# Two visits per group at fixed FFN steps, stores on SP's queue, and a last group in halves, in a fused linear-attention and FFN kernel

## The chip, the cores and the metric

The kernel runs on one core of a Trainium2 chip. The metric is the device time of one execution, in microseconds (us). TensorE is called PE here, VectorE DVE, ScalarE ACT, GpSimd POOL and SyncE SP. PEld is the stream of weight loads of PE.

## The reference

Per batch and head a gated linear attention keeps a 48x48 state that decays by `alpha` and takes in one outer product per token. Its output, 3072 tokens by 384 features, goes through a two-layer feed-forward network (FFN) with an exact GELU.

```
state = zeros((B, H, D, D))                      # B 4, H 8, S 768, D 48
for t in range(S):
    state = alpha[:, :, t, :, None] * state + einsum('bhd,bhe->bhde', k[:, :, t], v[:, :, t])
    y[:, :, t] = einsum('bhd,bhde->bhe', q[:, :, t], state)
x = y.transpose(0, 2, 1, 3).reshape(3072, 384)
h = x @ w_in                                     # 384 x 2048
g = 0.5 * h * (1 + erf(h / sqrt(2)))
return g @ w_out                                 # 2048 x 384
```

## The kernel before

The tokens form 12 groups of 256, three to a batch, and each group has two units (u = 0 and 1), each with half of the heads, so there are 24 units. All arithmetic is float32; every factor of a large matmul is split in a high and a low part, so a product takes three matmuls.

**The attention of a unit.** DVE scans the decays forward (`pp`, line 283) and backward (`rp`, 304) and scales the keys (`akq`, 309). POOL scales the queries (`qk`, 299). PE then makes the scores (`scores`, 325). DVE masks them (`ss`, 340) and ACT copies their other part (`kn`, 334). PE writes the product inside chunks (`inside`, 399), the state sums (`sums`, 426) and the part outside chunks (`outside_part`, 487) into one PSUM tile, `ybank`. DVE adds the sums up to states (`chain`, 452 and 454). ACT casts the finished `ybank` to the high half of the FFN's input (`x_high`, 541) and DVE makes the low half (`x_low`, 545). After the last chunk of a batch no state is needed, so `chain` has three adds in the last group of a batch and four (the first may be a copy) elsewhere.

**A visit.** From unit 6 on, PE does its attention work in bundles: the visit of unit n holds `inside` of n, `sums` of n+1, `scores` of n+2 and `outside_part` of n, in this order. `inside` and `outside_part` write to one bank from different row tiles. For that reason a POOL memset of one column (`done`, 834), called the fence, waits for the sums and `outside_part` waits for the fence.

**The FFN.** A group takes 8 steps f = 0 to 7. Step f is `gemm1` (18 matmuls into `hp`, 572), two GELUs on ACT (`ghi`, 593, and in place on `hp`, 594), their difference on DVE (`glo`, 599), and `gemm2` (12 matmuls into two accumulators `acc` of 128 tokens, 620; the first 8 need only `ghi`, the last 4 need `glo`). The two `hp` buffers let the next `gemm1` run while ACT and DVE work. There is one pair of accumulators, so step 0 of a group waits in `gemm2` until DVE has copied the pair of the group before to `part` (639). A store then carries `part` to the output (645), on POOL's queue; for the last group on SP's and ACT's queues (641).

**The order.** A planner at build time plays all engines through with a table of costs (`COST`) and writes out the order of PE, DVE, ACT and SP; POOL's order follows the program. On PE an operation marked `late` (the visits) is taken when what it waits for has been done for at least `MARGIN`; otherwise FFN steps run. At run time each engine works through its list in this fixed order and waits on semaphores.

A last check (`total`, 1088) reads whether all decays are in the range that the fast path allows.

Of the kernel before, what the change touches and what calls it, by code (L numbers as in the profile page):

```python
# [30 lines left out]
LANES = 8  # L31
RATE, ALONE, LATENCY, SMALL, BEGIN = 350e3, 290e3, 2.1, 50e3, 2.2
MARGIN = 1.5
HOME = {0: 0, 1: 1, 2: 2, 4: 1, 5: 0, 6: 2, 8: 1, 9: 0, 10: 2, "s": 1}
X_GAP, Z_GAP, HI_GAP, LO_GAP, LATE_GAP = (128, 0, 192), 0, (64, 0), (0, 64), 0
COST = dict(
    scan=0.65, back=0.72, keys=0.65, q=1.35, qv=0.62, scores=1.0, kn=0.5, mask=0.62, inside=1.05, chain=1.15, outer=0.85, carry=0.26, last=0.34, last_p=0.15, sums=0.55, scaled=0.45,
    xh=0.6, xl=0.65, spread=0.62, check=0.95, load=0.46, fetch=0.46, u=0.92, c0=0.56, c1=0.9, c2=0.45, c3=0.95, c4=0.92,
    hi=0.84, lo=0.9, gemm1=2.12, gelu=0.58, minus=0.35, low=0.63, gemm2=2.1, part=1.1,
)  # L40
ORDER = "0 1 2 3 a b c d 4 e 5 f g 6 h 7 i j k l 8 m n o p"

# [2 lines left out]
def gla_then_gelu_ffn(ctx: ExitStack, tc: tile.TileContext, q, k, v, alpha, akq, w_in, w_out, out):  # L45
    nc = tc.nc
    B, H, D, S = q.shape
    NF, P, NK, _ = w_in.shape
    DM, DFF = NK * P, NF * P
    NT = B * S  # L50
    C = 128
    G = 2 * C
# [8 lines left out]
    NG = B * GPB  # L61
    NSB = GPB
# [34 lines left out]
    minus = const.tile([P, P], F32R, name="minus")  # L97
# [29 lines left out]
    done = const.tile([P, 64], F32, name="done")[:, :1]  # L127
# [13 lines left out]
    for half in range(2):  # L141
        r = slice(half * CS, (half + 1) * CS)
        nc.gpsimd.affine_select(
            out=mask[r],
# [10 lines left out]
    wi_hi, wi_lo, wo_hi, wo_lo = (  # L155
        [const.tile([P, 2, DM], F32R, name=f"{n}{f2}") for f2 in range(NF2)] for n in ("wih", "wil", "woh", "wol")
    )
# [189 lines left out]
    def turned_over(g, b):  # L347
        return g >= NSB and b == 1
# [125 lines left out]
    def outside_part(g, u):  # L474
        d = cur[g, u]
        for c in range(NCH // 2):
            for i in range(2):
                for bb, h in ((0, 0), (0, 1), (1, 0), (1, 1)):
                    b = bb if g >= NSB else bb ^ h
                    j = 2 * c + b  # L480
                    if g % GPB == 0 and j == 0:
                        continue
                    r = slice(h * DP, h * DP + D)
                    o0 = (h ^ turned_over(g, b)) * DP
                    o = slice(o0, o0 + D)
                    t = (2 * i + c) * CS
                    ins = nc.tensor.matmul(  # L487
                        ybank[o, b, t : t + CS],
                        lhsT=states[u][j][r, i],
                        rhs=d["qs"][r, i, j, :CS],  # L490
                        start=False,
                        stop=True,
                        skip_group_check=True,
                    )
                    tc.add_manual_dep(
                        ins.ins,
                        (d["chain"] if g < NSB else d["fence"]).ins.name,
                        mybir.DependencyInfo(mybir.DependencyClass.Sync, mybir.DependencyReason.DATA),
                        reason="row tiles of one bank",
                    )  # L500
# [3 lines left out]
    def x_tiles(g):  # L504
# [4 lines left out]
        else:  # L509
            if g in range(XB):  # L510
                gap(ffn, X_GAP[HOME[g]], f"gap_x{g}")
            x = ffn.tile([P, NK, 2, G], F32R, tag=f"x{HOME[g]}", bufs=1, name=f"x{g}")
        xt[g] = x[:, :, 0], x[:, :, 1]
# [99 lines left out]
    started = set()  # L613

    def gemm2(g, f, ghi, glo, acc, first, last, done, n0=None):
        for k in range(2):
            for t in range(2):
                for j in range(2):
                    for a, w in (((ghi, wo_hi[f]), (ghi, wo_lo[f])), ((glo, wo_hi[f]),))[k]:
                        nc.tensor.matmul(  # L620
                            acc[t],
                            lhsT=a[:, j, t * C : (t + 1) * C],
                            rhs=w[:, j, :],
                            start=(first and j == 0 and k == 0 and w is wo_hi[f]),
                            stop=(last and j == 1 and k == 1),
                        )
        EARLY = tuple(range(NSB))
        if not last:
            return

        def evacuate():
            o = parts[0 if g == "s" else g % NSB]
            for t in range(2):
                if g in started:
                    nc.vector.tensor_tensor(out=o[:, t], in0=o[:, t], in1=acc[t], op=ALU.add)
                elif g in EARLY or t == 1 and g == NG - 1:
                    nc.scalar.copy(o[:, t], acc[t])
                else:
                    nc.vector.tensor_copy(o[:, t], acc[t])  # L639
                if g == NG - 1:  # L640
                    (nc.scalar if t else nc.sync).dma_start(out[g * G + t * C : g * G + (t + 1) * C, :], o[:, t])
            started.add(g)
            if done and g != NG - 1:
                rows = out[g * G : (g + 1) * G, :] if n0 is None else out[bass.ds(n0, G), :]
                nc.gpsimd.dma_start(rows.rearrange("(t p) e -> p t e", p=C), o)  # L645

        return evacuate

# [84 lines left out]
    n_units = NG * NU  # L733

    class Op:
        made = 0

        def __init__(self, eng, cost, fn, deps=(), rank=0.0, moves=()):
            self.eng, self.name, self.cost, self.fn, self.rank, self.moves = eng, cost, COST[cost], fn, rank, moves
            self.late = False  # L740
            self.deps = [d for d in deps if d is not None]
            self.start = self.end = None
            self.n = Op.made
            Op.made += 1

# [15 lines left out]
    def op(*args, **kw):  # L761
        ops.append(Op(*args, **kw))
        return ops[-1]

    load, ready_x, unit, wops, x_last = {}, {}, {}, {}, {}
    gemms = {}

    def plan_unit(n):
        g, u = divmod(n, NU)
        d = unit[n] = {}  # L770
        p, pp_ = unit.get(n - 1, {}), unit.get(n - 2, {})
        r = unit_rank[n]
# [23 lines left out]
        e, cost = ("DVE", "qv") if pool else ("POOL", "q")  # L796
# [20 lines left out]
        if not pool:  # L817
            if n == NU * NSB:
                d["opening"] = op("PE", "scores", lambda: None, [p["xl"]], rank=r)
                d["opening"].parts = []  # L820
                d["opening"].cost = 1.6
                d["opening"].fn = lambda o=d["opening"]: [x() for x in o.parts]
            d["sums"] = d["opening"] if n == NU * NSB else p["visit"]
            d["sums"].deps += [d["kn"], d["v"], p["chain"]]
            d["sums"].parts.insert(0, lambda: sums(g, u))
            d["chain"] = op("DVE", "chain", lambda: chain(g, u), [d["sums"], pp_.get("carry")], rank=-1)
            d["visit"] = op("PE", "scores", lambda: None, [d["mask"], d["chain"], d["v"], p["xh"], p["xl"]], rank=r)
            d["visit"].parts = []

            def visit(o=d["visit"]):  # L830
                inside(g, u)
                for x in o.parts:
                    x()
                fence = nc.gpsimd.memset(done, 0.0)
                tc.add_manual_dep(
                    fence.ins,
                    cur["last"].ins.name,
                    mybir.DependencyInfo(mybir.DependencyClass.Sync, mybir.DependencyReason.DATA),
                    reason="row tiles of one bank",
                )  # L840
                cur[g, u]["fence"] = fence
                outside_part(g, u)

            d["visit"].fn = visit
            d["visit"].cost = 2.65 if n < n_units - 2 else 1.75
            d["inside"] = d["outer"] = d["visit"]
        else:
            d["inside"] = op("PE", "inside", lambda: inside(g, u), [d["mask"], d["kn"], d["v"], p.get("xh"), p.get("xl"), p.get("chain"), p.get("outer")], rank=r)
        for side in range(2):
# [29 lines left out]
        if u == NU - 1:  # L879
            part = P * 2 * G  # L880
# [28 lines left out]
    for n in range(n_units):  # L909
        plan_unit(n)  # L910
# [10 lines left out]
    def when(o):  # L921
        d = next((v for v in unit.values() if v.get("xh") is o), None) if o.name == "xh" else None
        at = o.at()
        if at is None or d is None:
            return at
        for dep in d["free"]:
            if isinstance(dep, tuple):
                dep = x_op(dep)
                if not dep:
                    return None  # L930
            if dep.end is None:
                return None
            at = max(at, dep.end + WAIT)
        return at
# [83 lines left out]
    def choose(e, t):  # L1018
# [5 lines left out]
        if e != "PE":  # L1024
            return best
        if best is not None and not (best.late and best.at() + MARGIN > t):
            return best
# [14 lines left out]
    t = 0.0  # L1042
    idle = 0
    while True:
        moved = False
        for e in ("DVE", "ACT", "PE", "SP", "POOL"):
            if free_at[e] <= t + 1e-9:
                o = choose(e, t)
# [11 lines left out]
    last = steps[-1]  # L1060
# [9 lines left out]
    first = min(o.start for o in plan if o.name == "gemm1")  # L1070
    early = sorted((o for o in plan if o.eng == "PE" and o.start <= first), key=lambda o: o.start)
    for o, after in zip(early, early[1:]):
        n = int((after.start - o.end - 0.3) / FILL)
# [77 lines left out]
```

## Time and profile before

| | before |
|---|---|
| median of 3 runs | 505.67 us (505.07 to 506.33) |
| the profiled execution, time | 506.43 us |
| its span, first to last instruction | 504.8 us |
| mean granted TensorE clock | 0.998 of full speed |
| PE busy | 488.3 us, 97% of the span |
| PEld busy | 475.1 us, 94% |
| DVE busy | 301.0 us, 60% |
| ACT busy | 218.2 us, 43% |
| POOL busy | 43.9 us, 9% |
| DVE busy from 172.2 to 227.0 us | 51.0 of 54.8 us |
| DVE busy from 227.0 to 371.0 us | 65.6 of 144.0 us |

The span lies 1.6 us under the time of the same execution; the rest is outside of the program's instructions. PE's busy share says that hardly any of the span is without a matmul, but matmuls are pipelined, and a stretch can be busy and still longer than it has to be. The last visits end at 369 us; from there to 499.2 us PE does FFN steps alone.

### The profile page before, as it was taken

What the parts mean: (1) busy time and instruction counts of PE and PEld (TensorE: products, weight loads), DVE (VectorE), ACT (ScalarE), POOL (GpSimd) and SP (SyncE); (2) the same over time, 40 slices, a digit from 0 to 9 for tenths busy, and PEclk for the clock granted to TensorE, in tenths of its full rate; (3) what the DMA queues carried; (4) which work ended last, traced back from release to release, by engine and by line L of the source; (5) the groups of instructions that cost most, each with busy time, mean ns of one, the idle gap of its engine ahead of it and who ended that gap; (6) DMA issues with size and microseconds to landing.
All of it is one profiled execution on the core that took longest, in us unless ns stands there. A gap on an engine that the chain in (4) does not pass through costs nothing.

```text
span 504.8 us, 13837 instructions
## 1 busy us (share of the span) xinstructions
PE 488.3 (97%) x5970; PEld 475.1 (94%) x5970; DVE 301.0 (60%) x579; ACT 218.2 (43%) x467; POOL 43.9 (9%) x80
## 2 busy tenths in 40 slices
PE   8898999999999999999999999999989999999995
PEld 8787889999999999998999999999989999999995
DVE  6999999999789999898366363251231211211211
ACT  2666865645455556544352352342322222222221
POOL 4000011000122121311020020000000000000000
PEclk9999999999999999999999999999999999999999
DMA  8956463531034444434030020010010000000001
GB/s 312 375 178 232 159 206 127 187 127 64 0 129 118 137 158 144 129 115 137 1 120 24 3 81 1 0 50 1 1 48 1 1 32 1 33 0 1 32 1 36
DMA packets 15250, 44.20 MB, mean 88 GB/s; under 512 B 2224, under 2 KB 5728, under 8 KB 15184
## 3 DMA queue, kind: packets, MB, share of 16 engines
q1 hardware_dynamic: 13520, 38.44, 22.6%
q0 software_dynamic: 1232, 4.33, 2.5%
q8 instruction: 49, 0.80, 0.7%
q10 hardware_dynamic: 432, 0.49, 0.4%
q14 instruction: 17, 0.14, 0.1%
HBM read 36.18 MB, written 4.72 MB: 81 GB/s over the span
## 4 chain that ended last, share of the span: by engine, by line
PE 74%; DVE 11%; issue 10%; ACT 2%; DMA 1%; ACTq 1%; POOL 0%; DVEq 0%; POOLq 0%
PE hp L572 33%; PE acc L620 33%; PE s L325 2%; DVE pp L283 2%; PE ybank L487 2%; PE warm L90 1%; PE ybank L399 1%; DVE rp L304 1%; PE ybank L426 1%; DMA akq<-in_akq_dram 1%; DVE x L545 1%; DVE part L639 1%; DVE ss L340 1%; DVE states L454 1%; PE ybank L367 1%
## 5 line engine op out<-in xcount | busy, mean ns | idle before, releaser
L572 PE MATMUL hp<-x,wih 128*128 128x256 f32 x1152 | 201.1, 277 | 1.1 <-issue 1.1
L572 PEld LDWEIGHTS hp<-x,wih 128*128 128x128 f32 x1152 | 178.1, 188 | 1.7 <-issue 1.3
L572 PE MATMUL hp<-x,wil 128*128 128x256 f32 x576 | 159.2, 276 | 0.0
L599 DVE TENSOR_TENSOR glo<-hp,ghi 128x512 fp32r<-128x512 f32 x92 | 63.1, 686 | 161.1 <-ACT hp L594 161.0
L593 ACT ACTIVATE ghi<-hp 128x512 fp32r<-128x512 f32 x96 | 57.3, 597 | 193.6 <-PE hp L572 193.4
L620 PE MATMUL acc<-woh,ghi 128*128 128x384 f32 x384 | 130.9, 341 | 0.0
L620 PE MATMUL acc<-wol,ghi 128*128 128x384 f32 x384 | 128.9, 336 | 0.0
L572 PEld LDWEIGHTS hp<-x,wil 128*128 128x128 f32 x576 | 108.2, 188 | 0.0
L620 PE MATMUL acc<-woh,glo 128*128 128x384 f32 x384 | 82.3, 335 | 1.0 <-DVE glo L599 1.0
L620 PEld LDWEIGHTS acc<-woh,ghi 128*128 128x128 f32 x384 | 72.1, 188 | 1.6
L620 PEld LDWEIGHTS acc<-wol,ghi 128*128 128x128 f32 x384 | 72.1, 188 | 0.0
L620 PEld LDWEIGHTS acc<-woh,glo 128*128 128x128 f32 x384 | 67.8, 188 | 1.6 <-DVE glo L599 1.3
L594 ACT ACTIVATE hp<-hp 128x512 f32<-128x512 f32 x96 | 56.9, 593 | 0.0
L304 DVE TENSOR_TENSOR_SCAN rp<-akq,rp,top 128x255 f32<-128x255 f32 x48 | 34.7, 753 | 0.8
L283 DVE TENSOR_TENSOR_SCAN pp<-akq,top 128x256 f32<-128x256 f32 x48 | 31.1, 680 | 3.8 <-POOL qk L299 2.0
L299 POOL TENSOR_TENSOR qk<-akq,pp 128x512 f32<-128x512 f32 x18 | 25.2, 1398 | 43.8 <-DVE pp L283 14.6
L645 POOL DMA_DIRECT2D out_dram<-part x11 | 8.4, 759 | 223.2 <-DVE part L639 209.3
L325 PE MATMUL s<-qk,akq 48*64 48x112 f32 x768 | 24.3, 260 | 1.6 <-PE ybank L487 1.0
L334 ACT COPY kn<-s 128x384 f32<-128x384 f32 x24 | 11.5, 481 | 29.5 <-DVE ss L340 16.3
L541 ACT CAST x<-ybank 64x256 fp32r<-64x256 f32 (+4 forms) x60 | 20.0, 333 | 9.9 <-PE ybank L487 5.5
L454 DVE TENSOR_TENSOR states<-ybank,states 128x96 f32<-128x96 f32 x66 | 16.8, 255 | 10.3 <-ACT x L541 8.3
L309 DVE TENSOR_TENSOR akq<-akq,rp 128x512 f32<-128x512 f32 x24 | 22.4, 932 | 0.7
(78 smaller groups left out, 412.7 us busy)
## 6 DMA issues: line engine op xcount, KB each, us to landing
akq<-in_akq_dram SPq DMA_DIRECT2D x22, 768.0 KB, 4.8
st<-in_moe_w_in_dram SPq DMA_DIRECT2D x8, 768.0 KB, 4.3
st<-in_moe_w_out_dram SPq DMA_DIRECT2D x8, 768.0 KB, 4.7
vn<-in_v_dram SPq DMA_DIRECT2D x12, 384.0 KB, 4.0
out_dram<-part POOLq DMA_DIRECT2D x11, 384.0 KB, 3.7
x<-z SPq DMA_DIRECT2D x63, 32.0 KB, 1.9
akq<-in_akq_dram SPq DMA_DIRECT2D x2, 512.0 KB, 4.6
akq<-in_akq_dram SPq DMA_DIRECT2D x2, 256.0 KB, 3.3
```

What stands on the lines that cost most here:

```text
L283: nc.vector.tensor_tensor_scan(pp[:, i], at[:, i], top, MID, ALU.mult, ALU.min)
L299: eng.tensor_tensor(out=qs[:, :, :, :CS], in0=by_chunk(qt), in1=by_chunk(pp), op=ALU.mult)
L304: nc.vector.tensor_tensor_scan(rp[:, i, G - 2 :: -1], at[:, i, G - 1 : 0 : -1], top[:, 1:], rp[:, i, G - 1 :], ALU.mult, ALU.min)
L309: nc.vector.tensor_tensor(out=kt, in0=kt, in1=rp, op=ALU.mult)
L325: nc.tensor.matmul(d["s"][o, h, e : e + KW], lhsT=d["kt"][r, i, t], rhs=d["qs"][r, i, j], start=True, stop=True)
L454: d["chain"] = nc.vector.tensor_tensor(out=st[j + 1], in0=new, in1=st[j], op=ALU.add)
L541: nc.scalar.copy(hi, y)
L572: nc.tensor.matmul(hp[:, j, :], lhsT=a[:, j, i * P : (i + 1) * P], rhs=x[:, i, :], start=(j == 0 and i == 0 and n == 0), stop=(i == NK - 1 ...
L593: nc.scalar.activation(ghi, hp, AF.Gelu)
L594: nc.scalar.activation(hp, hp, AF.Gelu)
L599: nc.vector.tensor_tensor(out=glo, in0=hp, in1=ghi.bitcast(F32), op=ALU.subtract)
L620: nc.tensor.matmul(acc[t], lhsT=a[:, j, t * C : (t + 1) * C], rhs=w[:, j, :], start=(first and j == 0 and k == 0 and w is wo_hi[f]), stop= ...
```

## The change

Four things change.

1. The visits of groups 5 to 11 get a fixed place: unit u of group g follows `gemm1` of step `VISITS[u]` (0 and 4) of group g-1. Before they came as soon as the `late` rule let them.
2. The last two visits (units 22 and 23, which have no `scores`) are split: `inside` in one place, then the fence, which the planner now knows, and `outside_part` as a PE operation of its own.
3. The stores of groups 0 to 10 go from POOL's queue to SP's.
4. In the last `gemm2` of the last group the matmuls are sorted by accumulator. The second accumulator is copied by DVE and ACT in halves of 192 columns and stored in two halves, on SP's and ACT's queues. In all other groups nothing changes in `gemm2`.

```diff
+VISITS = (0, 4)
...
     def gemm2(g, f, ghi, glo, acc, first, last, done, n0=None):
+        rounds = [(k, t) for k in range(2) for t in range(2)]
+        if done and g == NG - 1:
+            rounds.sort(key=lambda x: x[1])
+        for k, t in rounds:
...
                 else:
-                    nc.vector.tensor_copy(o[:, t], acc[t])
-                if g == NG - 1:
-                    (nc.scalar if t else nc.sync).dma_start(out[g * G + t * C : g * G + (t + 1) * C, :], o[:, t])
+                    rows = out[g * G + t * C : g * G + (t + 1) * C, :]
+                    half = DM // 2 if t else DM
+                    nc.vector.tensor_copy(o[:, t, :half], acc[t][:, :half])
+                    nc.sync.dma_start(rows[:, :half], o[:, t, :half])
+                    if t:
+                        nc.scalar.copy(o[:, t, half:], acc[t][:, half:])
+                        nc.scalar.dma_start(rows[:, half:], o[:, t, half:])
...
-                nc.gpsimd.dma_start(rows.rearrange("(t p) e -> p t e", p=C), o)
+                nc.sync.dma_start(rows.rearrange("(t p) e -> p t e", p=C), o)
...
-                outside_part(g, u)
+                if n < n_units - 2:
+                    outside_part(g, u)
             d["visit"].fn = visit
-            d["visit"].cost = 2.65 if n < n_units - 2 else 1.75
+            if g > NSB + 1:
+                d["visit"].after = (g - 1, VISITS[u])
+            d["visit"].cost = 2.65 if n < n_units - 2 else 0.85
             d["inside"] = d["outer"] = d["visit"]
+            if n >= n_units - 2:
+                fenced = op("POOL", "fence", lambda: None, [d["visit"]])
+                d["outer"] = op("PE", "outer", lambda: outside_part(g, u), [fenced], rank=r)
...
     def when(o):
+        if o.after is not None:
+            step = gemms.get(o.after)
+            if at is None or step is None or step.end is None:
+                return None
+            at = max(at, step.end)
```

The program's order is the same on PE up to `gemm1` of step 2 of group 3, and 14 visits (units 10 to 23) lie behind it in both. On PE the visit of unit 16, the first of group 8, stands before the change in the FFN of group 4, between `gemm1` and `gemm2` of step 3 (`hp` and `acc` carry the group and the step, `ss` the group and the unit):

```order
L572 MATMUL hp_4_3_3430<-x4_2279,wil3_149 128x256
L399 MATMUL ybank_137<-ss_8_0_3239,vn0_116 64x64 x16
L426 MATMUL ybank_137<-vn0_116,kn_127 64x48 x12
L325 MATMUL s_9_0_3482<-qk0_120,akq1_119 64x112 x16
L487 MATMUL ybank_137<-qk1_121,states0_131 48x64 x16
L620 MATMUL acc0_4_0_3215<-woh3_157,ghi_4_3_3516 128x384
```

After the change it stands three groups later, behind `gemm1` of step 0 of group 7 and ahead of the last `gemm2` of group 6:

```order
L573 MATMUL hp_7_0_4191<-x7_3798,wil0_146 128x256
L400 MATMUL ybank_137<-ss_8_0_3808,vn0_116 64x64 x16
L427 MATMUL ybank_137<-vn0_116,kn_127 64x48 x12
L326 MATMUL s_9_0_4238<-qk0_120,akq1_119 64x112 x16
L488 MATMUL ybank_137<-qk1_121,states0_131 48x64 x16
L623 MATMUL acc0_6_0_3841<-woh7_161,ghi_6_7_4186 128x384
```

The visit itself is the same; what moved is its place, from 8.7 us after the visit before it to some half a group after it. Between this visit and the next group's first `gemm2` PE now has one `gemm2` and one `gemm1`.

On DVE, with what each instruction waits for, the copies of the accumulators of group 3 (`part`) stood before the change between two scans of a later unit:

```order
L465 SCALAR_TENSOR_TENSOR states1_132<-states1_132,pe_6_1_2517 128x96
L283 SCALAR_TENSOR_TENSOR pp_8_1_3111<-akq0_117,top_113 128x256 [waits DMAHW7_49,Pool_49]
L639 COPY part0_173<-acc0_3_0_2437 128x384 [waits DMASW0_49,PE_49]
L639 COPY part0_173<-acc1_3_0_2438 128x384 [waits PE_49]
L283 SCALAR_TENSOR_TENSOR pp_8_1_3111<-akq0_117,top_113 128x256
```

After the change they stand behind the whole work that follows the visit of unit 10: the states of unit 11, the mask of unit 12 and the low half of group 5's input:

```order
L600 TENSOR_TENSOR glo_4_0_2795<-hp_4_0_2711,ghi_4_0_2792 128x512 [waits DVE_49,PE_49,Activation_49]
L455 TENSOR_TENSOR states1_132<-ybank_137,states1_132 128x96 [waits PE_49,Activation_49]
L455 TENSOR_TENSOR states1_132<-ybank_137,states1_132 128x96 [waits DVE_49] x2
L341 TENSOR_TENSOR ss_6_0_2818<-s_6_0_2758,mask_133 128x512 [waits Activation_49]
L546 TENSOR_TENSOR x5_2809<-ybank_137,x5_2809 128x2x2x64
L546 TENSOR_TENSOR x5_2809<-ybank_137,x5_2809 64x2x2x64 x2
L642 COPY part0_173<-acc0_3_0_2437 128x384 [waits PE_49]
L642 COPY part0_173<-acc1_3_0_2438 128x384 [waits PE_49]
L284 SCALAR_TENSOR_TENSOR pp_7_0_2867<-akq1_119,top_113 128x256 [waits DMAHW1_49,Pool_49]
```

The first add of the states waits for PE and for ACT. The same order stands at the visits of units 12, 14, 16, 18 and 20.

The end of the program on DVE and on ACT after the change, with the waits:

```order
L646 COPY part2_175<-acc0_11_0_6103 128x384 [waits DMAHW2_49,PE_49]
L646 COPY part2_175<-acc1_11_0_6104 128x192 [waits PE_49]
...
L649 COPY part2_175<-acc1_11_0_6104 128x192 [waits DMAHW2_49,DVE_49]
L650 DMA out_0_dram<-part2_175 128x192 [waits DMAHW3_49,Activation_49]
```

ACT's half copy waits for DVE, whose half of the same accumulator stands ahead of it; before, ACT copied the whole second accumulator and waited for PE.

## Rows read from the trace of the kernel before

**Rows 1.** Waits, whole run: who waited for whom, us in total, times, longest.

```profile
PEld ybank L487 <- POOL done L834: 3.0, 7, 1.4
PE acc L620 <- DVE glo L599: 1.0, 1, 1.0
```

**Rows 2.** Timeline of PE from 171.9: start us, us, engine, line, operation, tiles, count.

```profile
172.18 0.39 PE L572 MATMUL hp<-x,wih 128*128 128x256 f32 x2
```

**Rows 3.** Timeline of all engines from 499; in brackets idle before and releaser.

```profile
498.83 0.34 PE L620 MATMUL acc<-woh,glo 128*128 128x384 f32 x1
...
499.20 0.48 ACT L637 COPY part<-acc 128x384 f32<-128x384 f32 x1 [3.08 <-PE acc L620]
...
499.71 0.39 ACTq L641 DMA_DIRECT2D out_dram<-part  x1
```

**Rows 4.** The chain that ended last, from 225: start us, us, what.

```profile
375.32 2.09 PE acc L620 x12
...
490.87 2.08 PE acc L620 x12
```

**Rows 5.** Timeline of PE, 254 to 264 us: one visit between FFN steps.

```profile
254.21 0.44 PE L620 MATMUL acc<-woh,ghi 128*128 128x384 f32 x1
...
260.59 0.69 PE L399 MATMUL ybank<-ss,vn 64*64 64x64 f32 x32
...
261.56 0.96 PE L325 MATMUL s<-qk,akq 48*64 48x112 f32 x32
262.35 0.62 PE L487 MATMUL ybank<-qk,states 48*48 48x64 f32 x24
262.90 0.44 PE L620 MATMUL acc<-woh,ghi 128*128 128x384 f32 x1
```

**Rows 6.** Timeline of POOL, 155 to 180 us.

```profile
157.64 0.75 POOL L645 DMA_DIRECT2D out_dram<-part  x1 [6.06 <-DVE part L635]
...
176.81 1.30 POOL L299 TENSOR_TENSOR qk<-akq,pp 128x512 f32<-128x512 f32 x1 [1.12 <-DMA x<-z]
```

**Rows 7.** Timeline of DVE, 173 to 180 us.

```profile
173.24 0.69 DVE L309 TENSOR_TENSOR akq<-akq,rp 128x512 f32<-128x512 f32 x1
...
175.15 0.17 DVE L287 TENSOR_SCALAR pe<-pp 128x2 f32<-128x2 f32 x1
...
176.98 1.67 DVE L309 TENSOR_TENSOR akq<-akq,rp 128x512 f32<-128x512 f32 x1
178.58 0.68 DVE L599 TENSOR_TENSOR glo<-hp,ghi 128x512 fp32r<-128x512 f32 x1
```

**Rows 8.** Timeline of all engines, 291.9 to 299.8 us: a visit of a unit u = 1.

```profile
291.95 0.65 PE L487 MATMUL ybank<-qk,states 48*48 48x64 f32 x24
...
293.50 0.82 ACT L541 CAST x<-ybank 128x128 fp32r<-128x128 f32 x3
...
294.36 1.13 DVE L454 TENSOR_TENSOR states<-ybank,states 128x96 f32<-128x96 f32 x4 [3.62 <-ACT x L541]
...
296.00 0.90 DVE L545 TENSOR_TENSOR z<-ybank,z 128x128 fp32r<-128x128 f32 x3
...
299.36 0.17 DVE L287 TENSOR_SCALAR pe<-pp 128x2 f32<-128x2 f32 x1
```

**Rows 9.** Timeline of ACT, 207 to 216 us: the cast after a visit u = 0.

```profile
211.83 1.14 ACT L541 CAST x<-ybank 128x256 fp32r<-128x256 f32 x3 [1.45 <-PE ybank L487]
```

**Rows 10.** Timeline of DVE, 324 to 336 us.

```profile
324.35 1.29 DVE L545 TENSOR_TENSOR x<-ybank,x 128x256 fp32r<-128x256 f32 x3 [0.37 <-ACT x L541]
...
328.04 1.02 DVE L639 COPY part<-acc 128x384 f32<-128x384 f32 x2
```

**Rows 11.** DMA issues, whole run: count, KB each, median us from issue to landing.

```profile
out_dram<-part SPq DMA_DIRECT2D x1, 192.0 KB, 2.3
out_dram<-part ACTq DMA_DIRECT2D x1, 192.0 KB, 3.0
```

**Rows 12.** Line L1146: count, duration ns min/median/max, first and last start us.

```profile
L1146 SPq EVENT_SEMAPHORE  x14: 17/28/28, 502.8 to 504.7; - x14
```

More of the change, by code (lines that the diff above doesn't have):

```diff
@@ L38 @@
     xh=0.6, xl=0.65, spread=0.62, check=0.95, load=0.46, fetch=0.46, u=0.92, c0=0.56, c1=0.9, c2=0.45, c3=0.95, c4=0.92,
-    hi=0.84, lo=0.9, gemm1=2.12, gelu=0.58, minus=0.35, low=0.63, gemm2=2.1, part=1.1,
+    hi=0.84, lo=0.9, gemm1=2.12, gelu=0.58, minus=0.35, low=0.63, gemm2=2.1, part=1.1, fence=0.7,
 )
@@ L615, in gemm2 @@
     def gemm2(g, f, ghi, glo, acc, first, last, done, n0=None):
[L616 to L626, printed above, removed]
+        rounds = [(k, t) for k in range(2) for t in range(2)]
+        if done and g == NG - 1:
+            rounds.sort(key=lambda x: x[1])
+        for k, t in rounds:
+            for j in range(2):
+                for a, w in (((ghi, wo_hi[f]), (ghi, wo_lo[f])), ((glo, wo_hi[f]),))[k]:
+                    nc.tensor.matmul(
+                        acc[t],
+                        lhsT=a[:, j, t * C : (t + 1) * C],
+                        rhs=w[:, j, :],
+                        start=(first and j == 0 and k == 0 and w is wo_hi[f]),
+                        stop=(last and j == 1 and k == 1),
+                    )
         EARLY = tuple(range(NSB))
@@ L635, in evacuate @@
                     nc.vector.tensor_tensor(out=o[:, t], in0=o[:, t], in1=acc[t], op=ALU.add)
-                elif g in EARLY or t == 1 and g == NG - 1:
+                elif g in EARLY:
                     nc.scalar.copy(o[:, t], acc[t])
-                else:
-                    nc.vector.tensor_copy(o[:, t], acc[t])
-                if g == NG - 1:
-                    (nc.scalar if t else nc.sync).dma_start(out[g * G + t * C : g * G + (t + 1) * C, :], o[:, t])
+                elif g != NG - 1:
+                    nc.vector.tensor_copy(o[:, t], acc[t])
+                else:
+                    rows = out[g * G + t * C : g * G + (t + 1) * C, :]
[5 more added lines that the diff above has]
+                        nc.scalar.dma_start(rows[:, half:], o[:, t, half:])
             started.add(g)
@@ L742, in __init__ @@
             self.start = self.end = None
+            self.after = None
             self.n = Op.made
```

## The prediction

> **What bounds the kernel now.** I read the page first: PE is busy 97% of the span, no other engine is above 60%. Then the waits: PE itself hardly waits in what the change reaches; weight loads and a matmul wait 3.0 us for POOL's fence in 7 waits, the longest 1.4, so the other six share 1.6, about 0.27 each, and one `gemm2` waits 1.0 us for `glo` [rows 1]. So the kernel is a row of PE work without holes, and the time is counted on PE from the point where the order changes to the last matmul: from 172.18, the start of `gemm1` of step 2 of group 3 [rows 2], to 498.83 + 0.34 = 499.17 [rows 3], together 326.99 us. What follows it, 5.6 us to the end of the span, is the tail.
>
> The chain of work gives the price of an FFN step where nothing else runs: from 375.32 to 490.87 it has 28 steps of one `gemm2` and one `gemm1`, 115.55 / 28 = 4.127 us, of which 2.09 is `gemm2` [rows 4]. By the order 70 steps lie in the stretch, 288.9 us. So 326.99 - 288.9 = 38.1 us belong to the 14 visits and to what PE waits around them.
>
> A visit with nothing in its way: from the first matmul of one `gemm2` (254.21) to the first of the `gemm2` behind the visit (262.90) are 8.69 us, with one `gemm2` and two `gemm1` in them, 2.09 + 2 x 2.04 = 6.17. The visit costs 2.52; its own matmuls take 262.90 - 260.59 = 2.31, so going in and out costs 0.21 [rows 5].
>
> **Part by part.**
>
> *Fixed places.* Twelve whole visits at 2.52 are 30.2 us, wherever they stand, if nothing is late.
>
> *Split visits.* `inside` and sums take 261.56 - 260.59 = 0.97, `outside_part` 0.55 for 24 rows of the view, some 0.6 for 32 [rows 5]. Unit 22 needs 0.97 + 0.6; unit 23 has no sums, half of 0.97 + 0.6; four pieces go in and out, 4 x 0.21 = 0.84; the matmul of the range check, which stood within a visit, now does so alone, 0.3 by the same 0.21. Together 3.8 (bounds 3.4 and 4.3). So without new waits the 14 visits cost 34.0, **-4.1** against 38.1. The fence no longer holds PE here: a `gemm2` of 2.09 lies between both halves, and the longest wait, 1.4, was one of the two.
>
> *Stores.* On POOL a store waits for its `part` and then takes 0.75 us; the fence stands behind it [rows 6]. The late fences after 172 are in the 38.1. One more is ahead of it, the store at 157.64: **-0.3** (0 to -0.4). On SP the stores stand ahead of loads of `akq` and the spreads of `x`. The copy a store waits for is done some 5 us after its visit, and the next spread on SP comes a half group, about 16 us, later: nothing, and were that cover gone, each us of delay beyond it would be a us at the start of a group.
>
> *What is late next.* Without the visit at 174.31, PE reaches the last 4 of the 12 matmuls of `gemm2` of step 2, group 3, at 172.18 + 2 x 2.04 + 8/12 x 2.09 = 177.65. DVE is there in a backlog that the change leaves in place: its key product starts at 176.98 and takes 1.67 beside POOL's query product (176.81), against 0.69 for the one at 173.24 without it. That query product waits for the visit and goes; so `glo` starts 0.6 after 176.98 and ends 0.68 later, 178.26 [rows 6, 7]. PE waits **+0.65** (0, if DVE comes earlier, to 1.6, if the product stays long).
>
> *After each visit u = 0* PE does one `gemm2` and one `gemm1`, then wants the accumulators. With E the end of `outside_part`, that is E + 4.15 (a step of 4.13, begun 0.07 before E, and half of the 0.21). DVE does first, by the order, states, mask and low half. What it waits for is seen at the visit of 291.95: E is 292.60, and DVE, idle since long, starts the states at 294.36, 0.04 after ACT's cast ended at 294.32, although the sums were done before the scores [rows 8]. For u = 0 the cast takes 1.14 [rows 9]. So: start of cast E + 0.07, cast 1.14, wake 0.03, states and mask 296.00 - 294.36 = 1.64 [rows 8], low half 1.25 of the 1.29, first copy 0.55 of the 1.02 for two [rows 10]: E + 4.7. PE waits 0.55; where the states have three adds, 0.29 less, 0.26. By the order four visits have four (units 12, 14, 18, 20), two have three (10, 16): 2.7, taken as **+2.6** (0, if the states didn't wait for the cast, to 4.5, at a slip of 0.3 each). The second copy comes 0.47 after the first, within the 0.7 that the first four matmuls take (4/12 of 2.09).
>
> A rule speaks to that wait. The Trainium skill, page "PSUM — Partial Sum Buffer", section "PSUM bank collisions raise a hardware error", says that two engines may not touch one bank in the same partitions at once, not even both to read, so software has to order them. Cast and states read different columns of one tile; if the rule made the wait, it holds at u = 0 too, as in my sum; if the row at 294.36 were chance, the sum would be 2.6 lower.
>
> *After each visit u = 1* PE does two `gemm2` and two `gemm1`; in the next `gemm2` it wants `glo` at E + 0.05 + 2 x 2.09 + 2 x 2.04 + 1.39 = E + 9.7 (the first starts 0.07 before E [rows 5], the visit's exit slows it by half of the 0.21). DVE: states at E + 1.76, up to the scan's end 299.36 - 294.36 = 5.00 [rows 8], backward scan to keys 176.98 - 175.15 = 1.83, keys 0.6, `glo` 0.68 [rows 7]: E + 9.9. That is 0.2 late at the two visits that have four adds and a carried state (units 13, 19); elsewhere it just fits: **+0.4** (0 to 4.9, if POOL's query product met the keys at five of them, 1.67 - 0.69 each).
>
> *The end.* Last matmul M = 499.17. Before: ACT's copy of 0.48 to 499.68, its store issued at 499.71, landing 3.0 later at M + 3.5 [rows 3, 11]. After: two copies of 192 columns; the listing has ACT wait for DVE, so they stand in a row, 0.36 + 0.32 by the columns, issue at M + 0.8. A store of 96 KB with another of 96 KB beside it: the one of 192 KB with a free start landed in 2.3, so 2.2 (1.95, if half the data saves half of the 0.7 by which 3.0 exceeds 2.3, to 3.0). Landing M + 3.0, **-0.5** (-0.9 to +0.3). By the same page and rule the halves could not be copied at once, since they lie in one bank; no row here shows two engines in one bank. Without it the end would come 0.36 earlier.
>
> After the landing SP goes through 14 semaphore instructions from 502.8 on [rows 12]. I take it that eight of them are for POOL's DMA semaphores, which the change leaves unused, at some 0.06 each: **-0.5** (0 to -0.5).
>
> **Sum.** -4.1 - 0.3 + 0.65 + 2.6 + 0.4 - 0.5 - 0.5 = -1.75. The profiled execution took 506.43 (span 504.8), 0.8 over the median; so 504.7 for such a run, and **503.9 us** against the median of 505.67.
>
> **The rivals.**
>
> *A: the states don't wait for the cast.* For it: the adds depend on PE's sums alone by the algorithm. Against it: the 0.04 us in [rows 8]. Then 2.6 and the 0.4 go: 503.9 - 3.0 = 500.9.
>
> *B, slower: POOL's queries meet DVE's keys.* At 176.98 such a meeting made the keys 1.67 instead of 0.69 [rows 7]. After a visit u = 1 the `glo` behind the keys has no slack, so a meeting costs 0.98 at each of five visits, 4.9 less the 0.4 counted: 503.9 + 4.5 = 508.4. It decides if POOL's product starts later than 7 us after a visit; against it: before, it followed the visit by about 1 us, and the keys now come 8.6 after it.
>
> *C: it doesn't do what it says at the end.* The two stores of halves land no sooner than one whole (+0.5), the final semaphores stay (+0.5), and the waits after u = 0 come out 0.1 longer each (+0.6): 505.5, no change.
>
> **Chances.** The forecast 0.64, by its own range 502.6 to 505.2; A 0.14; B 0.08; C 0.14. Below 0.3% (1.5 us) a measurement of this kernel can't tell a change from none; 503.9 lies 0.25 beyond that line, so of the forecast 0.38 is faster and 0.26 the same. Faster 0.38 + 0.14 = 0.52, same 0.26 + 0.14 = 0.40, slower 0.08. The range 501.6 to 505.5 holds the forecast, most of C and little of A, about 0.8.
>
> **What would show it.** PE's stretch from step 2 of group 3 to the last matmul about 0.5 us shorter than 326.99, and no wait for `done`; a wait of 0.65 for `glo` near 177; waits of 0.3 to 0.55 for `part` at six group starts; the states 0.04 behind ACT's cast each time. ACT's half copy right behind DVE's, the last landing 3.0 after the last matmul, and some 6 instead of 14 semaphore instructions at the end. No wait for `part` would make A right, keys of 1.6 beside a POOL product B, and a tail of 5.6 us C.

## The result and the profile after

The changed kernel takes 508.35 us (median of 6 runs, 508.06 to 508.81) against 505.48 us (505.07 to 506.33, 6 runs) for the kernel before: ratio 1.0057, 95% interval 1.0045 to 1.0069. It is slower by 0.57%; the forecast was 503.9.

| stretch of the profiled executions, us | before | after | change | forecast |
|---|---|---|---|---|
| start to first visit (138.92 and 138.26) | 138.92 | 138.26 | -0.66 | 0 |
| to `gemm1` of step 2, group 3 (172.18 and 172.42) | 33.26 | 34.16 | +0.90 | -0.3 |
| to the end of the last matmul (499.17 and 502.36) | 326.99 | 329.94 | +2.95 | -0.45 |
| to the end of the span (504.75 and 506.65) | 5.59 | 4.29 | -1.30 | -1.0 |

The first row has the same code in both. So the end went as forecast and a little better, and the loss lies in the stretch of the visits and just ahead of it. What PE waits for there (the view of waits: us in total, times, longest) answers to [rows 1]:

```profile
PEld acc L623 <- DVE glo L600: 3.4, 6, 1.3
PE acc L623 <- DVE part L642: 3.0, 6, 0.6
PE acc L623 <- DVE glo L600: 1.5, 2, 1.0
```

PE no longer waits for `done`; it waits for `part` at six group starts, as forecast, and for `glo` more often than forecast. The wait for `part` is best seen at the visit of unit 12, on PE (the visit, then `gemm2`, `gemm1` and the next group's first `gemm2`), on ACT and on DVE:

```profile
236.81 0.69 PE L400 MATMUL ybank<-ss,vn 64*64 64x64 f32 x32
...
239.12 0.44 PE L623 MATMUL acc<-woh,ghi 128*128 128x384 f32 x1
...
241.33 0.39 PE L573 MATMUL hp<-x,wih 128*128 128x256 f32 x2
...
244.06 0.41 PE L623 MATMUL acc<-woh,ghi 128*128 128x384 f32 x1 [0.54 <-DVE part L642]
```

```profile
239.23 1.13 ACT L542 CAST x<-ybank 128x256 fp32r<-128x256 f32 x3 [1.22 <-PE ybank L488]
```

```profile
240.40 0.26 DVE L453 COPY states<-ybank 128x96 f32<-128x96 f32 x1 [1.67 <-ACT x L542]
240.69 0.84 DVE L455 TENSOR_TENSOR states<-ybank,states 128x96 f32<-128x96 f32 x3
241.45 0.68 DVE L341 TENSOR_TENSOR ss<-s,mask 128x512 f32<-128x512 f32 x1
242.05 1.28 DVE L546 TENSOR_TENSOR x<-ybank,x 128x256 fp32r<-128x256 f32 x3
243.36 1.02 DVE L642 COPY part<-acc 128x384 f32<-128x384 f32 x2
```

DVE is idle for 1.67 us, starts the states 0.04 after ACT's cast ends, and comes to the copies of the accumulators 4.2 us after the visit (its last matmul ends at 239.19); the first is done at about 243.92 (0.56 each), and PE restarts at 244.06. That is the chain which the prediction drew.

The row that the table has at +0.90 is one place near 158, on DVE and POOL, before the change and then after it, where DVE and PE go on with `glo`:

```profile
158.60 1.39 DVE L304 TENSOR_TENSOR_SCAN rp<-akq,rp,top 128x255 f32<-128x255 f32 x2
...
159.34 1.74 POOL L299 TENSOR_TENSOR qk<-akq,pp 128x512 f32<-128x512 f32 x1 [0.84 <-PE ybank L487]
```

```profile
157.72 2.50 DVE L305 TENSOR_TENSOR_SCAN rp<-akq,rp,top 128x255 f32<-128x255 f32 x2
...
158.37 1.30 POOL L300 TENSOR_TENSOR qk<-akq,pp 128x512 f32<-128x512 f32 x1 [1.09 <-PE ybank L488]
...
160.14 0.66 DVE L600 TENSOR_TENSOR glo<-hp,ghi 128x512 fp32r<-128x512 f32 x1
...
160.85 0.97 PE L623 MATMUL acc<-woh,glo 128*128 128x384 f32 x4 [0.99 <-DVE glo L600]
```

With the store gone from POOL's queue the fence runs 1.30 after the visit's start instead of 1.86, and the visit takes 0.31 less, as forecast; POOL's query product follows it and is early too. It now falls on DVE's second backward scan: the two scans take 2.50 instead of 1.39, `glo` comes late and PE waits.

At the end (the timeline, then the DMA issues: count, KB each, median us to landing) the halves stand in a row, ACT behind DVE, as forecast:

```profile
502.40 0.36 DVE L646 COPY part<-acc 128x192 f32<-128x192 f32 x1 [0.49 <-PE acc L623]
502.79 0.32 ACT L649 COPY part<-acc 128x192 f32<-128x192 f32 x1 [3.48 <-DVE part L646]
503.14 0.39 ACTq L650 DMA_DIRECT2D out_dram<-part  x1
```

```profile
out_dram<-part SPq DMA_DIRECT2D x1, 192.0 KB, 2.4
out_dram<-part SPq DMA_DIRECT2D x1, 96.0 KB, 1.9
out_dram<-part ACTq DMA_DIRECT2D x1, 96.0 KB, 1.8
```

The last landing is 503.14 + 1.8, some 2.6 after the last matmul (before 3.5 by [rows 3, 11]), and SP's final rows are 10 instead of 14 [rows 12], where the prediction has some 6.

### The profile page after: what moved, and what is told of

Its sections match the earlier page's. It is cut to its first block, busy times and chain, and to the rows that moved or that the text cites. A ratio compares the mean times of both kernels' runs of the same rounds, so it can differ in the third digit from the quotient of the medians.

```text
span 506.6 us, 13804 instructions
## 1 busy us (share of the span) xinstructions
PE 490.6 (97%) x5970; PEld 476.3 (94%) x5970; DVE 297.4 (59%) x580; ACT 219.0 (43%) x467; POOL 33.8 (7%) x69
## 4 chain that ended last, share of the span: by engine, by line
PE 83%; DVE 9%; ACT 4%; issue 2%; DMA 1%; ACTq 0%; SPq 0%; DVEq 0%
PE acc L623 36%; PE hp L573 35%; PE s L326 3%; PE ybank L488 3%; PE ybank L400 3%; PE ybank L427 2%; ACT x L542 2%; DVE x L546 2%; DVE states L455 1%; DVE rp L305 1%; DVE ss L341 1%; DVE pp L284 1%; DMA akq<-in_akq_dram 1%; DVE part L642 1%; PE spare L1089 1%
## 5 line engine op out<-in xcount | busy, mean ns | idle before, releaser
L300 POOL TENSOR_TENSOR qk<-akq,pp 128x512 f32<-128x512 f32 x18 | 23.5, 1307 | 45.9 <-DVE pp L284 15.6
L326 PEld LDWEIGHTS s<-qk,akq 48*64 48x64 f32 x768 | 19.7, 133 | 2.5 <-PE ybank L488 1.0
L546 DVE TENSOR_TENSOR x<-ybank,x 64x256 fp32r<-64x256 f32 (+3 forms) x54 | 19.1, 355 | 2.0 <-ACT x L542 1.1
```

Of the source, the lines that this page charges most:

```text
L300: eng.tensor_tensor(out=qs[:, :, :, :CS], in0=by_chunk(qt), in1=by_chunk(pp), op=ALU.mult)
L326: nc.tensor.matmul(d["s"][o, h, e : e + KW], lhsT=d["kt"][r, i, t], rhs=d["qs"][r, i, j], start=True, stop=True)
L546: nc.vector.tensor_tensor(out=lo, in0=y, in1=hi.bitcast(F32), op=ALU.subtract)
```

## The experiments

T1 is the theory that the trace after suggests: the fixed places cost what DVE delivers late after a visit, 4.6 us of copies and 1.3 us of `glo`. T2 and T3 are rivals that the expectations name. Ratios are to the kernel before, with 95% intervals; its median was 505.15 to 505.50 in the several sets of runs.

**Stores back on POOL.**

```
-                nc.sync.dma_start(rows.rearrange("(t p) e -> p t e", p=C), o)
+                nc.gpsimd.dma_start(rows.rearrange("(t p) e -> p t e", p=C), o)
```

> The changed kernel with one edit taken back: the stores of groups 0 to 10 stand on POOL's queue again; the order on PE, DVE and ACT is unchanged. Theory T1 (the loss is made by the fixed places: copies of the accumulators that come late after the first visit of a group, 4.6 us, and glo that comes late after the second, 1.3 us): these waits stay. Near 157 the fence stands behind a store again (+0.3) and POOL's query product comes later, so that it no longer meets DVE's backward scan (-1.2); at the end the semaphore instructions come back (+0.5). 508.35 - 0.4 = about 508, between 507.3 and 508.6, ratio to the kernel before 1.004 to 1.006. Theory T2 (the stores on SP make the loss, by moving POOL's products forward onto DVE's work): the loss goes, 505.5 or less, ratio 1.000.

Measured 508.42 us, ratio 1.0059 (1.0044 to 1.0074): T2 falls, the stores are worth nothing here on balance. The trace shows two effects that cancel. Near 158 POOL (first two rows) and DVE stand as in the kernel before:

```profile
156.75 0.76 POOL L654 DMA_DIRECT2D out_dram<-part  x1 [6.06 <-DVE part L638]
...
158.45 1.74 POOL L300 TENSOR_TENSOR qk<-akq,pp 128x512 f32<-128x512 f32 x1 [0.84 <-PE ybank L488]
```

```profile
157.71 1.39 DVE L305 TENSOR_TENSOR_SCAN rp<-akq,rp,top 128x255 f32<-128x255 f32 x2
```

The scans take 1.39 again and it is the product, started later, that is stretched (1.74 against 1.30). From that visit to the next are 9.07 us here and 9.96 after the change, so 0.9 is saved, and the tail from the last matmul is 5.33 against 4.29, so 1.0 is lost, with 14 final rows on SP instead of 10.

**Copies ahead of the low half.** The planner is told that the states wait for the cast:

```
             d["chain"] = op("DVE", "chain", lambda: chain(g, u), [d["sums"], pp_.get("carry")], rank=-1)
+            if n > NU * (NSB + 2):
+                d["chain"].deps.append(p["xh"])
```

> The changed kernel, with the states of a unit made to wait in the planner for ACT's cast, as they do on the chip. PE keeps its order and the visits their places; on DVE the copies of the accumulators now stand behind states and ahead of the low half, the mask and the carried state ahead of the states, and half a forward scan goes into the time of the cast after the second visit. T1: the copy is done some 2.9 us after the visit of u = 0 where PE asks for it at 4.15, so the six waits go (-4.6); of the five late glo of 0.25 most go too (-0.6 to -1.3). 508.35 - 5.5 = 502.9, between 502.4 and 503.8, ratio 0.993 to 0.997. T3 (the places themselves cost it, by longer going in and out or by slower FFN steps, whatever DVE's order): at least 507, ratio 1.003 or more.

Measured 502.12 us, ratio 0.9942 (0.9925 to 0.9960), a little more of a gain than T1's 502.4 to 503.8. No wait for `part` is left, and of the waits for `glo` two remain, those near 158 and 176, ahead of the first fixed visit (197.68). DVE at the visit of unit 12, where PE asks for the accumulators at 242.26:

```profile
239.79 0.84 DVE L455 TENSOR_TENSOR states<-ybank,states 128x96 f32<-128x96 f32 x3
240.55 1.01 DVE L642 COPY part<-acc 128x384 f32<-128x384 f32 x2
241.48 1.28 DVE L546 TENSOR_TENSOR x<-ybank,x 128x256 fp32r<-128x256 f32 x3
```

The distance of visits says what the waits had cost. First matmuls of three visits (u = 0, 1, 0), after the change and here:

```profile
236.81 0.29 PE L400 MATMUL ybank<-ss,vn 64*64 64x64 f32 x4
256.63 0.29 PE L400 MATMUL ybank<-ss,vn 64*64 64x64 f32 x4
276.01 0.29 PE L400 MATMUL ybank<-ss,vn 64*64 64x64 f32 x4
```

```profile
235.71 0.29 PE L400 MATMUL ybank<-ss,vn 64*64 64x64 f32 x4
254.74 0.29 PE L400 MATMUL ybank<-ss,vn 64*64 64x64 f32 x4
273.75 0.29 PE L400 MATMUL ybank<-ss,vn 64*64 64x64 f32 x4
```

Here both distances are 19.03 and 19.01, four steps of 4.127 and a visit of 2.52 as the prediction has them; after the change they are 19.82 and 19.38. The six distances behind a visit u = 0 lost 4.56 in all, the five behind u = 1 lost 1.36. T3 falls: a fixed place as such costs nothing. One thing went beyond the edit: PE's order did not stay quite the same, since in groups 4 to 8 `gemm2` of step 6 went ahead of `gemm1` of step 7.

**Visits at steps 1 and 5.** `VISITS = (1, 5)`.

> The changed kernel with the visits one step later, at steps 1 and 5. The copies of the accumulators now come ahead of the first visit of a group, with a gemm1 and no other work of DVE between. T1: the six waits for the copies go (-4.6); the first visit of a group now has the same steps behind it as the second, so its glo may be late too, by up to 0.25 at six visits (0 to +1.5). 508.35 - 4.6 + 0.7 = 504.5, between 503.6 and 505.4, ratio 0.996 to 1.000. T3 (fixed places as such cost it): no gain, 507.5 to 509, ratio 1.004 or more. Here T1 says that the place matters through the copies, where the run before leaves the place and moves the copies.

Measured 503.93 us, ratio 0.9969 (0.9955 to 0.9983), inside what T1 gave. The view of waits has no row for `part`, and the same late `glo` as after the change:

```profile
PEld acc L623 <- DVE glo L600: 3.4, 6, 1.3
```

So one step of distance removes the waits for the copies and leaves the others; the first visits of a group add no late `glo` of their own.

**No fixed places.** The two lines that set `after` are left out, the other three edits stay.

> The changed kernel without the fixed places: the visits come when the late rule lets them; stores on SP, split visits and halves stay. T1: the waits of 4.6, 1.3 and 0.8 that follow fixed visits go; some of the fence waits of the kernel before go as well, since no store stands ahead of a fence (1 to 2 of the 3.65 us); the tail stays 1.35 shorter than before, the loss near 157 stays (+0.9). 505.5 + 0.9 - 1.35 - 2.5 = 502.5, between 501.5 and 504, ratio 0.992 to 0.997. T2 (stores): 507 or more, ratio 1.003 or more, since POOL's products stay early.

Measured 503.05 us, ratio 0.9961 (0.9946 to 0.9975). The other three edits alone gain 2.4 us, and T2 falls a second time. The end is not shorter in this trace, though its last instructions are those of the changed kernel: the last landing comes 3.5 us after the last matmul, as before the change, since the halves land 3.1 and 2.3 us after their issue:

```profile
out_dram<-part SPq DMA_DIRECT2D x1, 96.0 KB, 3.1
out_dram<-part ACTq DMA_DIRECT2D x1, 96.0 KB, 2.3
```

The profile names no cause. In the six other runs with sorted matmuls and halves the last landing comes 2.5 to 2.9 after the last matmul.

**States ahead of the cast.** The two readers of the PSUM tile change places:

```
+            if n > NU * (NSB + 2):
+                p["xh"].deps.append(d["chain"])
```

> The changed kernel with the order of the two readers of PSUM after a visit turned round: ACT's cast waits for DVE's states (and not the states for the cast). PE's order is unchanged; the copies of the accumulators still stand behind states and mask, but ahead of the low half. T1 (the copies are late because the states stand behind the cast of 1.14 us): the states start within 0.1 us after the visit and end 1.1 after it, the mask at 1.75, the copy is done some 2.8 after the visit where PE asks for it at 4.15, and DVE gets 1.2 us back, so that glo after the second visit is on time too: 508.35 - 4.6 - 1.2 = 502.5, between 502.0 and 503.5, ratio 0.993 to 0.996. Rival (the states come 1.2 us after the visit for a reason of their own, such as the sums being readable late, and the cast before them is chance): the states still start some 1.2 after the visit, the cast ends 2.3 later, and the time is 505 or more.

Measured 502.35 us, ratio 0.9945 (0.9929 to 0.9960). DVE at the visit of unit 12 (its successor on PE starts at 238.60), then ACT:

```profile
238.71 0.26 DVE L453 COPY states<-ybank 128x96 f32<-128x96 f32 x1 [0.50 <-PE ybank L488]
239.00 0.84 DVE L455 TENSOR_TENSOR states<-ybank,states 128x96 f32<-128x96 f32 x3
...
240.66 1.02 DVE L642 COPY part<-acc 128x384 f32<-128x384 f32 x2
```

```profile
239.93 1.13 ACT L542 CAST x<-ybank 128x256 fp32r<-128x256 f32 x3 [1.16 <-DVE states L455]
```

The states now start right behind the visit, and it is the cast that waits for them. The sums were there all along; the 1.2 us were the order of the two readers. The Trainium skill, page "PSUM — Partial Sum Buffer", section "PSUM bank collisions raise a hardware error", says that two engines must not be in one bank and the same partitions at once, reads too, and that software has to keep them apart. Both orders here keep to it, the second reader 0.04 to 0.1 us behind the first; no run has the two at once, so what would happen then is not shown.

**Fixed places alone**, put into the kernel before.

> The kernel before with the fixed places alone: stores on POOL, whole last visits, whole last stores. T1 (the parts add up): the changed kernel's 508.35, without the earlier landing of halves (+0.9) and without the split of the last two visits (+1.2 by 2.01 + 2.56 + 0.3 before against 3.6 after); the stores are worth nothing on balance. 510.4, between 509.6 and 511.0, ratio 1.008 to 1.011. Rival T4 (the parts work on each other, the fixed places cost little with POOL's stores and whole visits): 508 or less, ratio 1.005 or less.

Measured 508.81 us, ratio 1.0069 (1.0051 to 1.0087), below the 509.6 to 511.0 that I gave. Most of the miss is the price of the whole last visits, which I took from the kernel before. There the last `outside_part` waited 1.27 for POOL's memset, which stood behind a store; here it waits 0.31. First the kernel before, then this one:

```profile
366.30 0.69 PE L399 MATMUL ybank<-ss,vn 64*64 64x64 f32 x32
368.27 0.66 PE L487 MATMUL ybank<-qk,states 48*48 48x64 f32 x32 [1.27 <-POOL done L834]
```

```profile
450.25 0.69 PE L400 MATMUL ybank<-ss,vn 64*64 64x64 f32 x32
451.25 0.67 PE L488 MATMUL ybank<-qk,states 48*48 48x64 f32 x32 [0.31 <-POOL done L836]
```

By the distances on PE the two whole visits take 4.0 us here and the split ones 3.76 after the change, so whole costs 0.25 and not 1.2. So the parts do not add up: the places alone cost 3.7, the rest alone gains 2.4, both together lose 2.9 and not 1.2. Most of the difference is the store's move, which is worth 1.1 without the places (below) and nothing with them (first run): there PE waits for the fence once, 0.3 us, and ahead of the fixed places, so these keep stores and fences apart anyway.

**No halves.** The second accumulator is copied and stored whole, the sorted matmuls stay:

```
-                    half = DM // 2 if t else DM
...
+                    if t:
+                        nc.scalar.copy(o[:, t], acc[t])
+                        nc.scalar.dma_start(rows, o[:, t])
```

> The changed kernel with the last group's second accumulator copied whole by ACT and stored whole on ACT's queue, as before; the sorted matmuls stay. If the halves save what the trace shows (issue 0.78 after the last matmul and landing 1.8 later, against 0.54 and 3.0), 508.35 + 0.95 = 509.3, between 508.9 and 509.6. By the value in the prediction (0.5) 508.85; if the stores on SP and not the halves made the tail shorter, 508.35.

Measured 508.14 us, ratio 1.0057 (1.0041 to 1.0073): a miss, the halves save nothing that medians tell. The DMA issues show why:

```profile
out_dram<-part ACTq DMA_DIRECT2D x1, 192.0 KB, 2.3
```

A whole store on ACT's queue lands in 2.3 us here and not in 3.0 as before. It is issued 0.96 us after SP's store instead of 0.27, since the sorted matmuls finish the first accumulator earlier. The last landing is 2.85 after the last matmul, against 2.61 with halves, a difference within what runs with the same end show (2.5 to 2.9).

**No sorted matmuls.** The two lines with `rounds.sort` are left out, the halves stay.

> The changed kernel with the matmuls of the last gemm2 in the old order; the copy and store in halves stay. If the shorter tail comes from the sorted order (the first accumulator's store starts 1 us before the second's, and the second's landing falls from 3.0 to 2.3 us, as in the run without halves), the halves are now issued right behind the whole store again and land later: 508.35 + 0.7 = 509.0, between 508.6 and 509.3. If the halves are what saved it, the landing stays some 1.9 after the issue and the time is 508.3. Below what a comparison of medians tells apart, so the landings in the trace decide.

Measured 509.22 us, ratio 1.0081 (1.0068 to 1.0094). The landings decide:

```profile
out_dram<-part ACTq DMA_DIRECT2D x1, 96.0 KB, 2.6
```

Half the data, issued 0.6 us after the whole store and 0.2 after SP's half, lands in 2.6, and 3.49 after the last matmul. With the 3.52 of the kernel before, the sort is worth 0.67 with whole stores (3.52 to 2.85) and 0.88 with halves (3.49 to 2.61), and the halves 0.03 without the sort and 0.24 with it. The medians agree: 0.9 between this run and the change, 0.2 between the run without halves and the change.

**Stores on SP alone**, in the kernel before.

> The kernel before with its stores of groups 0 to 10 on SP's queue and nothing else; the order on PE, DVE and ACT is unchanged. T1 (with visits where the late rule puts them, a store that waits for its copy stands ahead of fences, and moving it frees the fences; with fixed places there is nothing to free): the late fences go (-2.1: 0.2 to 0.3 at four visits, 0.3 ahead of 172 and 1.0 at the last visit), POOL's query product meets the scan near 158 (+1.2), the semaphores at the end go (-0.6 to -1.0). 505.3 - 1.7 = 503.6, between 503.0 and 504.3, ratio 0.994 to 0.998. Rival (a store move is worth nothing anywhere, as in the first run): 505.3, ratio 1.000.

Measured 504.07 us, ratio 0.9974 (0.9964 to 0.9984), inside T1's interval. The waits for the fence fall from 3.0 in 7 to this, while near 158 PE loses 1.3 as after the change (the visits there are 9.95 apart, where a visit and its steps take 8.69):

```profile
PEld ybank L487 <- POOL done L834: 0.7, 2, 0.4
```

**Copies first, and two `glo` ahead of scans.** The second run's edit, and in the planner's choice for DVE:

```
+        if e == "DVE" and best is not None and best.name in ("back", "keys") and HOLD[0] < t < HOLD[1]:
+            for o in waiting[e]:
+                if o.name == "low" and when(o) is not None and when(o) <= t + 0.45:
+                    return o if when(o) <= t + 1e-9 else None
```

> The run with the copies first (502.1), and besides, in the planner's stretch from 150 to 185 us, DVE keeps backward scans and key products back when a glo is due within 0.45 us; so the two glo that still come late, near 158 (1.39 lost) and 176 (0.78 lost), stand ahead of a scan. T1 (what is left of the loss is these two waits): 502.1 - 2.2 = 499.9, between 499.5 and 500.9, ratio 0.988 to 0.991. Rival (the scans and keys that are put back make a later visit late by as much): 501.5 to 502.5.

Measured 500.51 us, ratio 0.9910 (0.9895 to 0.9925), inside T1's range and the best of all. Near 176 PE's order changed too (one `gemm2` stands where two stood in a row), so what `glo` ahead of a scan is worth by itself is seen at 158 alone. There `glo` now stands between the two scans, and the second is stretched by POOL's product where nobody waits for it:

```profile
157.62 0.75 DVE L306 TENSOR_TENSOR_SCAN rp<-akq,rp,top 128x255 f32<-128x255 f32 x1
158.29 0.67 DVE L601 TENSOR_TENSOR glo<-hp,ghi 128x512 fp32r<-128x512 f32 x1
158.87 1.25 DVE L306 TENSOR_TENSOR_SCAN rp<-akq,rp,top 128x255 f32<-128x255 f32 x1
```

## Why the prediction was wrong

What held: twelve visits at 2.52, no wait for `done` after 172, the states 0.04 behind the cast, the copy done at E + 4.7 (243.92 with E = 239.19), the wait for `glo` near 177 (0.78 against 0.65), a shorter end. What failed are three terms of the sum; of the first two the mechanism was in the text and the size was wrong, of the third the mechanism was missing.

- **"+2.6" after each visit u = 0** measured 4.56, the upper end of its range (4.5). The step took the time until the copy is done as the loss, 0.55. Each of the four visits with four adds lost 0.77 to 0.82: PE needs another 0.14 from the end of the copy to its first matmul, and the first matmuls after a stop run some 0.1 later than in a row without one. The two visits with three adds were to lose 0.26: the first, at 198, lost 0.54; the other, at 315, lost 0.84, since PE started 0.43 after the copy's end, for which the profile names no cause.
- **"+0.4" after each visit u = 1** measured 1.36. I had three of five visits "just fit". They don't: all five lost 0.14 to 0.38, of the size of that same restart, which the prediction leaves out here too.
- **"Stores -0.3"** measured +0.9 up to 172. The fence came early as forecast. That POOL's query product, which follows the visit, comes early too is missing from the prediction, which asks for its meetings only with the key product and only after visits at fixed places. A backward scan reads two SBUF operands as well, and the pair took 1.39 before only because the product came later. The Trainium skill, page "SBUF — State Buffer", section "Who interferes with whom", says that a DVE instruction with two SBUF inputs and a GpSimd one that reads SBUF exclude each other, and that the one issued second waits. Both traces agree: after the change the scan is second (2.50 for the pair), with the stores on POOL the product is (1.74).
- **The end, "-0.5 and -0.5"**, measured -1.30: 0.91 by the landing, 0.38 by what follows it. The sum was near, the attribution was not: the landing gained 0.67 to 0.88 by the sort, to which the prediction gives nothing, and 0.03 to 0.24 by the halves; four semaphore instructions went, not eight.
- **Split visits, "3.8"**, measured 4.1: 3.76 for the two visits (units 22 and 23 are 18.66 apart with four steps between), and 0.33 for the matmul of the range check, which the 3.8 had within it.

These make 1.96 + 0.96 + 1.2 - 0.3 + 0.3, with 0.13 for the `glo` near 177 and -0.66 from the stretch ahead of the change 3.6 of the 3.65 by which the span was missed (-1.75 against +1.9). Between medians the miss is 4.45. The other 0.8 is the conversion to 503.9: it took off 0.8 because the profiled execution of before lay so far over its median, and that of after lay only 0.1 over.

Of the rivals, A is refuted (the states do wait) and C too (the end did shrink), though one part of C, longer waits after u = 0, came true at three times its size. B's 508.4 is close to the result, but not its mechanism: after the visits u = 1 POOL's product is over before the keys, which take 0.69; the one meeting that cost time was elsewhere, with a scan.

That the cause of the loss is the order on DVE behind fixed visits is shown from three sides: moving the copies (502.12), turning the readers round (502.35) and moving the visits by a step (503.93) each take it away.

## What to carry to other kernels

When work is given a fixed place ahead of a point where another engine has something due, write out that engine's whole queue between the two, with the waits that its planner does not know; here one dependency that the planner did not know (states behind the cast) cost 6 us. Price a stall by the distance of two recurring instructions, not by the idle time shown or by the end of what is waited for. An edit that frees a queue moves everything behind it earlier: follow the next instruction on that queue to what it will meet.

## What the runs showed of the hardware

- The idle time in the timeline understates a stall of PE: 0.54 shown at 244.06, 0.79 lost by the distance of the visits. The shown one counts from the end of the last matmul before it (243.52), but in a row without a stop the next one would have begun at 241.33 + 2.04 = 243.37; and the `gemm2` behind the stop takes 2.19 instead of 2.09.
- DVE's small operation on the states is hit by POOL's product like the scans: 0.26 us alone (244.41 after the change), 1.27 beside it in the run with the copies first, where POOL's product runs from 238.18 to 239.48.

```profile
238.32 1.27 DVE L466 SCALAR_TENSOR_TENSOR states<-states,pe 128x96 f32<-128x96 f32 x1
```

- How long a store takes to land went with what was issued just ahead of it as much as with its size: 192 KB in 3.0 us at 0.27 us behind another (three runs), in 2.3 at 0.96 us (one run); 96 KB in 2.6 at 0.6 us behind 192 KB (one run), in 1.7 to 2.1 at 1.2 us behind it (six runs). A seventh run with that last spacing took 2.3, and SP's half in it 3.1 where the six others have 1.7 to 2.0, so a single landing can be off by 1 us.
- Moving the stores of groups 0 to 10 off POOL's queue shortened SP's final rows from 1.9 us (14 of them) to 1.3 (10). The time from the last landing to the end fell by 0.3 in the kernel before (2.07 to 1.77) and by 0.9 in the changed one (2.61 to 1.68); what makes the second larger is not shown.
- The stretch ahead of all changes ended (first visit in the table) anywhere from 136.98 to 138.92 in the profiled executions, so a single profile compares two of these kernels no closer than 1 to 2 us; the distance of the first two visits behind it is 8.88 to 8.92 in all twelve, and distances of visits are the safer measure.
